# Values of the attention stage in two scaled f16 parts made by VectorE, with a per-head scale found on the chip

## The chip, the cores and the metric

The kernel runs as one program on one NeuronCore of a Trainium2 chip. TensorE (PE) multiplies matrices and adds into PSUM; VectorE (DVE), ScalarE (ACT) and GpSimd (POOL) work element by element; SyncE (SP) issues nearly all transfers of the 16 DMA engines. Each engine works through one queue in order. The metric is device time in microseconds; the kernel before has a median of 976.02 us over three runs (972.43 to 976.55).

## The reference

Attention of 4 batches of 8 heads with 576 tokens and 64 columns per head, causal, with a decay that is a running sum of log f; then two MLPs with a squared ReLU on 2304 tokens, 512 wide, hidden 2048. All inputs are float32.

```
scores = q @ k.T / 8 + cum[:, None] - cum[None, :]      # cum = cumsum(log(clip(f)))
scores = where(causal, -1e9, scores)
attn = exp(scores - max) ; attn = attn / (sum(attn) + 1e-9)
x = (attn @ v) transposed to (2304, 512)
x = relu(x @ w_in)**2 @ w_out        # first MLP
y = relu(x @ w2_in)**2 @ w2_out      # second MLP
```

## The kernel before

**Precision by parts.** A float32 matrix is written as a high part and a low part of a faster type, and three products (high by high, high by low, low by high) are added in PSUM. In attention the probabilities are two f16 parts, and the values v were three parts that together hold all 24 bits: a bf16 part read out of v's own upper half words, and two remainders, made by two subtractions on POOL (`v_parts`, line 448). The product probabilities by values, called AV below (`av`, line 750), then had 15 matmuls per head: five blocks of keys by two probability parts, with a weight of 128 columns that holds two value parts (columns 0 to 63 of the result are folded with columns 64 to 127 afterwards), and five more matmuls with a 64-column weight for the third value part (`THIRD`).

**Stages.** The first 192 tokens of every head go through small shapes (`first_part`, `pair`). The other 384 tokens go through `unit(b, h)`, 32 times, one per batch and head. A unit loads q and k (`raw`), splits them (lines 659 to 674), multiplies scores (line 713), takes maxima (409, DVE), exponents (417, ACT), reciprocals (423, 426), writes the two f16 parts of the probabilities (432 on ACT, 439 on DVE), turns them with one transposing transfer into the single buffer `pt` (line 731, SP), does AV (750) and folds the result into X (766, 768). As there is one `pt`, the transfer of a unit waits until AV of the unit before it is done. v has two buffers, so v of a unit is loaded once AV two units earlier is done.

**The MLPs.** `mlp_a(g)` is the first MLP on 256 tokens (lines 861 and 936: runs of 12 matmuls of 256 columns), nine groups g = 0 to 8. Groups 0 to 2 need only the first 192 tokens of each head, the later ones the units, so these runs fill TensorE between the steps of the units. When the last unit is folded, the second MLP's weights are prepared (`w_in_forms`, `w_out_parts`), and the second MLP (1233, 1259) ends the kernel.

**Order.** Nothing is timed at run time. `Plan.run` lays every engine's queue out beforehand: each step has a priority, a modelled duration and dependencies, and the planner issues on each engine the ready step of lowest priority number. A DMA step is given a modelled landing time. `either(...)` gives a step to whichever of two engines the planner finds free. The q and k load of unit h of the first batch may not start before a step of the first MLP whose number is P10 + P11*h (`TUNE`).

Of the kernel before, what the change touches and what calls it, by code (L numbers as in the profile page):

```python
# [22 lines left out]
NB = 13  # L23
MW = 448

THIRD = ((0, 0), (1, 1), (3, 0), (2, 1), (4, 0))
S15 = 2.0 ** -15


TUNE = dict(  # L30
    AP0=0.0, AP1=201.48, BP0=1647.15, BP1=207.89, P10=15.97, P11=1.88, P20=24.71, P21=3.44, P30=32.76,
    P31=1.6, P40=50, P41=6, PP=917.52, SP0=44.13, SP1=155.02, WP0=-459.53, WP1=133.32, e3=12, e6=6, ev=0,
    f3=2, f4=1, fa=0, fo=20.89, hl=3, kd=0, kl=3, la=0.1, nbo=2, nph=2, npt=1, nqa=3, pha=0, phi=2,
    pq=-119.59, pz=12.35, qd=2, ql=3, sqa=2, sqe=7, vd=-20.75, vr=2, wf=0.59, wl=3, wn=1, wq=2, ws=5,
# [29 lines left out]


class Op:
    __slots__ = ("how", "prio", "uses", "nwait", "ready", "outs", "data", "turn", "dmas", "rows")


class Plan:  # L70
# [14 lines left out]
    def __init__(self):  # L85
        self.ops = []

    def op(self, eng, dur, fn, prio, deps=(), uses=(), data=None, other=None, dmas=1, rows=128):


        o = Op()
        o.how, o.uses, o.data, o.dmas, o.rows, o.turn = {eng: (dur, fn, 0)}, tuple(uses), data, dmas, rows, dur == self.TURN[0]
# [12 lines left out]

    def run(self):
# [5 lines left out]
        lanes, issued = [0.0] * 8, 0  # L112
# [7 lines left out]
        todo = len(self.ops)  # L120
        t, events = 0.0, []
        while todo:
            again = True
            while again:
                again = False
                for e in engs:
# [38 lines left out]
                    if e == "PE":  # L165
# [65 lines left out]
def dve(n):  # L231
    return 0.07 + n / 960.0
# [30 lines left out]
def attention_then_two_squared_relu_mlps(  # L263
# [26 lines left out]
    P = Plan()  # L290
    op = P.op
# [12 lines left out]
    X = base.tile([128, KD, RING], F32, name="X")  # L304
# [11 lines left out]
    st_ = [st[:, 0:1024], st[:, 1024:2048]]  # L316
# [41 lines left out]
    def groups(c0, c1):  # L358
# [4 lines left out]
    ap_ = att_stack.enter_context(tc.tile_pool(name="att", bufs=1))  # L363
# [9 lines left out]
    vv_t = tiles(ap_, 2, [128, 5, 2, D], F32, "vv")  # L373
    VV = Pool(vv_t, True)
    stat = ap_.tile([128, 2, 3, 8], F32, name="stat")
    PP = Pool([(x, stat[:, i, 0], stat[:, i, 1], stat[:, i, 2])
               for i, x in enumerate(tiles(ap_, 2, [128, S], F32, "pp"))], True)

# [24 lines left out]
    all_att = []  # L403
# [39 lines left out]
    def v_parts(vv, n, prio, dep):  # L443


        def rest(eng, i):
            x = vv()[:, :, i]
            eng.tensor_tensor(out=vv()[:, :, 1] if i == 0 else x.bitcast(BF16)[:, :, 0::2], in0=x,  # L448
                              in1=x.bitcast(BF16)[:, :, 1::2], op=ALU.subtract)
# [4 lines left out]
        return dep  # L454

    vv_of = {}

    def first_part(y, prio):

# [183 lines left out]
    def unit(b, h, prio, first):  # L643

        c = QA
        qk_ = [Buf(QK), Buf(QK)]
        ta, tb = qk_
        raw, vv, ph, pT, o = Buf(RAW), Buf(VV), Buf(PH), Buf(PT), Buf(BO)
        vv_of[vv] = vv

        def load_raw():
            nc.sync.dma_start(out=raw(), in_=qk[b, h])
# [41 lines left out]
        ]  # L694

        def load_v():
            nc.sync.dma_start(out=vv()[:, :, 0], in_=v[b, h])

        ov = op("SP", P.COPY[0], load_v, prio + TUNE["vd"], [ld], [vv], data=0.91)
        ov = v_parts(vv, 5, prio + TUNE["vd"], ov)  # L700

        p_ops = []
        for t, blk in PB.items():
            pp = Buf(PP)
            q0, wd = QB[t], QB[t + 1]
            cuts = [(0, wd)] if wd <= 512 else [(0, wd // 2), (wd // 2, wd)]
# [18 lines left out]
            a = (pp, ph, t, 128, 0, wd, blk)  # L725
# [7 lines left out]
        o_tr = op("SP", P.TURN[0], tr, prio, p_ops + (a_av if b == 0 else []), [ph, pT], data=2.9)  # L733


        def av():
            x, w_, z = pT(), vv().bitcast(BF16), o()
            cuts = []
            for j in range(5):
                t = max(2, j)  # L740
                cuts.append((j, slice(QB[t] - QA, S - QA), slice(PB[t] + j, PB[4] + j + 1, 4)))
            todo = []
            for j, q, n in cuts:
                for z0 in range(0, 2 * NB, NB):
                    todo.append((z[:, q], w_[:, j].rearrange("p z d -> p (z d)")[:, 1::2], x[:, n.start + z0:n.stop + z0:n.step]))
# [12 lines left out]
        def fold(eng):  # L758
            s = p0
            rows = slice((h % 2) * 64, (h % 2) * 64 + 64)  # L760
            while s < p1:
                r = s % RING
                n = min(p1 - s, RING - r)
                dst = X[rows, h // 2, r:r + n]
                if eng == "ACT":
                    nc.scalar.mul(out=dst, in_=o()[64:128, s - p0:s - p0 + n], mul=S15)
                else:
                    nc.vector.scalar_tensor_tensor(
                        out=dst, in0=o()[0:64, s - p0:s - p0 + n], scalar=S15, in1=dst, op0=ALU.mult, op1=ALU.add)
# [11 lines left out]
    decoded = []  # L781
# [501 lines left out]
    with tc.manual_schedule():  # L1283
# [97 lines left out]
        o = op("SP", P.COPY[0], f_load, U, data=0.2)  # L1381
# [10 lines left out]
        o = op("DVE", dve2(Q0), lambda: f_clip(0, Q0), U, [o_f])  # L1392
# [20 lines left out]
        def step(n):  # L1413
            return m2_of[0, int(n) // NF, int(n) % NF]

        w_all = []
# [108 lines left out]
```

## Time and profile before

| | |
|---|---|
| median of three runs | 976.02 us (972.43 to 976.55) |
| profiled execution | 977.94 us, its span 976.2 us |
| PE busy | 948.3 us (97%) |
| DVE, ACT, POOL busy | 683.6, 453.1, 361.4 us (70%, 46%, 37%) |
| units: first AV to last AV | 150.84 to 482.62 us |
| TensorE clock | 0.77 of full up to 60 us, 1.00 for most of the rest |

The span counts from the first to the last instruction; the profiled execution has 1.7 us around it. Busy times of an engine are the union of its instructions. A wait is put down to what came last.

### The profile page before, as it was taken

Reading aid. Unit: us, or ns where it says so; the run is one execution under the profiler, and the core shown is the slowest. Engines: PE = TensorE matmul, PEld = TensorE weight load, DVE = VectorE, ACT = ScalarE, POOL = GpSimd, SP = SyncE. Lnnn points to the kernel's source line nnn. Section 1 sums busy time; section 2 is a strip of 40 time slices with the busy share of each in tenths; the row PEclk is TensorE's granted clock in tenths of the full one; section 3 lists DMA queues with packets and bytes.
Section 4 is the critical chain, followed back from the end, with each engine's and each line's share of the span. In section 5 each row is a group of like instructions: output and inputs, shape, how many; then the busy total and the mean of one; then the engine's idle time right before and its main releaser. Section 6 shows DMA issues by size and latency. Waiting matters only on the chain.

```text
span 976.2 us, 17134 instructions
## 1 busy us (share of the span) xinstructions
PE 948.3 (97%) x6463; PEld 866.7 (89%) x6463; DVE 683.6 (70%) x1341; ACT 453.1 (46%) x900; POOL 361.4 (37%) x315
## 2 busy tenths in 40 slices
PE   6999999999999999999999999999999999999997
PEld 3888898999997999999999998988898988989886
DVE  7998667787768778876478689888874445734343
ACT  3686677777777678775333353223230112311011
POOL 2244443444434435434232435332351314522130
PEclk7799999999999999999999999999999999999999
DMA  8767245666656756755546524674452111322113
GB/s 251 253 202 207 83 104 119 140 129 146 132 110 134 148 122 134 143 118 120 120 160 207 173 82 157 199 242 159 134 171 88 64 65 65 117 86 79 65 65 108
DMA packets 177187, 131.91 MB, mean 135 GB/s; under 512 B 140944, under 2 KB 155536, under 8 KB 175056
## 3 DMA queue, kind: packets, MB, share of 16 engines
q1 hardware_dynamic: 176848, 130.32, 49.1%
q8 instruction: 51, 0.84, 0.4%
q10 hardware_dynamic: 256, 0.49, 0.2%
q14 instruction: 32, 0.26, 0.1%
HBM read 85.07 MB, written 18.42 MB: 106 GB/s over the span
## 4 chain that ended last, share of the span: by engine, by line
PE 70%; DVE 11%; issue 9%; POOL 3%; ACT 3%; DMA 2%; POOLq 0%; SPq 0%; ACTq 0%; DVEq 0%
PE yp L936 16%; PE hp L861 16%; PE hp L1233 13%; PE bk L1259 10%; PE bk L750 5%; PE yp L1259 5%; PE bk L713 4%; POOL g L1246 2%; DVE ph L439 1%; DVE tmp L818 1%; DVE tmp L820 1%; DVE pp L409 1%; DVE w L1122 1%; POOL gt L886 1%; DVE w L837 1%
## 5 line engine op out<-in xcount | busy, mean ns | idle before, releaser
L936 PE MATMUL yp<-gt,w 128*128 128x256 f32 x1728 | 231.6, 283 | 1.8 <-POOL gt L886 1.7
L861 PE MATMUL hp<-xk,w 128*128 128x256 f32 x1728 | 227.7, 282 | 1.1 <-DVE w L837 0.8
L936 PEld LDWEIGHTS yp<-gt,w 128*128 128x128 f32 x1728 | 216.5, 189 | 6.2 <-POOL gt L886 3.1
L861 PEld LDWEIGHTS hp<-xk,w 128*128 128x128 f32 x1728 | 215.3, 190 | 3.0 <-DVE w L837 1.0
L886 POOL TENSOR_TENSOR gt<-sq,gt 128x512 fp32r<-128x512 f32 x72 | 97.3, 1352 | 154.4 <-ACT gt L883 135.9
L1259 PE MATMUL bk<-w,g 128*128 128x512 f32 x576 | 148.5, 394 | 0.7 <-POOL g L1246 0.7
L1246 POOL TENSOR_TENSOR g<-r,g 128x768 fp32r<-128x768 f32 x36 | 66.8, 1855 | 203.2 <-ACT g L1245 199.3
L1233 PE MATMUL hp<-w 128*128 128x384 f32 x630 | 123.9, 335 | 0.1
L1259 PEld LDWEIGHTS bk<-w,g 128*128 128x128 f32 x576 | 106.6, 188 | 18.7 <-POOL g L1246 1.6
L1245 ACT CAST g<-r 128x768 fp32r<-128x768 f32 x47 | 39.3, 835 | 180.1 <-DVE r L1244 180.0
L1233 PEld LDWEIGHTS hp<-w 128*128 128x128 f32 x630 | 111.7, 188 | 8.1 <-DVE st L1210 0.4
L417 ACT ACTIVATE pp<-pp,stat 128x448 f32<-128x448 f32 (+1 forms) x128 | 78.4, 613 | 44.6 <-DVE stat L409 37.0
L439 DVE SCALAR_TENSOR_TENSOR ph<-pp,stat,ph 128x320 f16<-128x320 f32 (+2 forms) x96 | 77.3, 814 | 15.5 <-ACT ph L432 13.9
L1210 DVE TENSOR_TENSOR r<-hp,st 128x384 f32<-128x384 f32 x62 | 34.5, 556 | 62.8 <-PE hp L1233 62.7
L448 POOL TENSOR_TENSOR vv<-vv 128x320 f32<-128x320 f32 x64 | 54.4, 850 | 54.8 <-DMA vv<-in_v_dram 42.1
L1244 DVE SCALAR_TENSOR_TENSOR r<-r 128x768 f32<-128x768 f32 x47 | 73.6, 1567 | 1.4
L1259 PE MATMUL yp<-w,g 128*128 128x512 f32 x288 | 74.5, 393 | 0.0
L1233 PE MATMUL hp<-w,far 128*128 128x384 f32 x378 | 74.1, 335 | 0.0
L870 ACT ACTIVATE sq<-hp 128x512 f32<-128x512 f32 x72 | 42.8, 594 | 66.8 <-PE hp L861 66.3
L1233 PEld LDWEIGHTS hp<-w,far 128*128 128x128 f32 x378 | 67.3, 188 | 4.7
L409 DVE CUSTOM_DVE_ANT_0 pp<-bk,mask 128x448 f32<-128x448 f32 (+1 forms) x128 | 59.4, 476 | 15.3 <-PE bk L713 9.9
L873 DVE SCALAR_TENSOR_TENSOR sq<-hp,sq 128x512 f32<-128x512 f32 x64 | 44.0, 688 | 35.1 <-ACT sq L870 34.7
(171 smaller groups left out, 1281.5 us busy)
## 6 DMA issues: line engine op xcount, KB each, us to landing
w<-wo_d SPq DMA_DIRECT2D x48, 512.0 KB
stage<-in_w_dram SPq DMA_DIRECT2D x26, 512.0 KB
raw<-in_qk_dram SPq DMA_DIRECT2D x32, 288.0 KB
wo_d<-part SPq DMA_DIRECT2D x16, 512.0 KB
ph<-in_w_dram SPq DMA_DIRECT2D x7, 1024.0 KB
st<-in_w_dram SPq DMA_DIRECT2D x6, 1024.0 KB
vv<-in_v_dram SPq DMA_DIRECT2D x32, 160.0 KB
qk_a<-in_qk_dram SPq DMA_DIRECT2D x16, 192.0 KB
```

The costliest lines, as they stand in the source:

```text
L409: nc.vector.tensor_tensor_reduce(out=x[:rows, c0:c0 + wd], in0=src, in1=msk, scale=-0.125, scalar=3.0e38 if first else nmax[:rows, 5:6], o ...
L417: nc.scalar.activation(out=x, in_=x, func=AF.Exp, scale=-1.0, bias=nmax[:rows, t:t + 1], accum_out=ssum[:rows, t:t + 1])
L439: nc.vector.scalar_tensor_tensor(out=flat[:rows, z:z + wd], in0=x, scalar=r, in1=flat[:rows, 128 * blk:128 * blk + wd], op0=ALU.mult, op1= ...
L448: eng.tensor_tensor(out=vv()[:, :, 1] if i == 0 else x.bitcast(BF16)[:, :, 0::2], in0=x, in1=x.bitcast(BF16)[:, :, 1::2], op=ALU.subtract)
L750: nc.tensor.matmul(dst.rearrange("p (n c) -> p n c", n=rh.shape[1]), lhsT=lt, rhs=rh, start=(i == 0), stop=(i == len(todo) - 1), skip_grou ...
L861: nc.tensor.matmul(ps, lhsT=lt, rhs=rh, start=(k_ == 0 and c == 0), stop=(k_ == KD - 1 and c == 2))
L886: eng.tensor_tensor(out=gt[1]()[:, :c], in0=sq()[:, :c], in1=f32(gt[0]()[:, :c]), op=ALU.subtract)
L936: nc.tensor.matmul(yp[d // 2]()[:, d % 2], lhsT=lt, rhs=rh, start=(i == 0 and c == 0 and d % 2 == 0), stop=(i == NF - 1 and c == 2), skip_ ...
L1233: nc.tensor.matmul(ps()[:, 0:TH], lhsT=lt, rhs=rh, start=(k_ == 0 and c == 0), stop=(k_ == 1 and c == 2))
L1244: o = op("DVE", dvs(TU), lambda r=r: nc.vector.scalar_tensor_tensor(out=r(), in0=r(), scalar=0.0, in1=r(), op0=ALU.max, op1=ALU.mult), e0, ...
L1246: l = either_vp(TU, lambda e, r=r, g=g: e.tensor_tensor(out=g()[:, 1], in0=r(), in1=f32(g()[:, 0]), op=ALU.subtract), e0, [h], [r, g])
L1259: nc.tensor.matmul(bank(ob[c]), lhsT=g()[:, a, c * 128:(c + 1) * 128], rhs=rw()[:, b], start=(p == 0 and x == 0 and z == 0), stop=(p == NP ...
```

## The change

v is written as two f16 parts. So that f16's range suffices, each head is first scaled by a power of two found from its largest magnitude: `scales(b)` loads all of v of a batch (2560 columns on 128 partitions, in five pieces; three for the first batch), takes the maximum of each row on DVE, stores 128 maxima to DRAM, reads them back onto all partitions, and in six small DVE steps makes a scale up and a scale down for each head. A unit's `v_parts` is then two DVE steps (multiply and round to f16; multiply and subtract). AV loses its five 64-column matmuls, and the two fold steps multiply with the scale down in place of the constant. The planner's DMA steps get an extra modelled landing time `lag`: 4 us for the pieces and for the reading back, 8 us for the store. P10 goes from 15.97 to 12.

```diff
-    AP0=0.0, AP1=201.48, BP0=1647.15, BP1=207.89, P10=15.97, P11=1.88, ...
+    AP0=0.0, AP1=201.48, BP0=1647.15, BP1=207.89, P10=12, P11=1.88, ...
...
-                            end = lanes[issued % 8] = dma + self.LAT["DMA"] + (self.TURNED if o.turn else 0.0)
+                            end = lanes[issued % 8] = dma + self.LAT["DMA"] + (self.TURNED if o.turn else 0.0) + o.lag
...
-        for i in range(2):
-            dep = either(TUNE["vr"], ("POOL", pool_(n * D), lambda i=i: rest(nc.gpsimd, i)),
-                         ("DVE", dvs(n * D), lambda i=i: rest(nc.vector, i)), prio, [dep], [vv_of[vv]])
+        def hi():
+            nc.vector.tensor_scalar(out=parts_v(vv)[:, :, 0], in0=x(), scalar1=up, scalar2=None, op0=ALU.mult)
+
+        def lo():
+            nc.vector.scalar_tensor_tensor(out=parts_v(vv)[:, :, 1], in0=x(), scalar=up, in1=parts_v(vv)[:, :, 0], op0=ALU.mult, op1=ALU.subtract)
+
+        o = op("DVE", dve(5 * D) + 0.07, hi, prio, [dep, scale_of[b]], [vv])
+        return op("DVE", dvs(5 * D) + 0.08, lo, prio, [o], [vv])
...
+    def scales(b, prio, pieces, space, deps):
...
+            o = op("SP", P.COPY[0], load, prio, deps + [os_[j - 2] if j > 1 else None], data=n * 0.00143, lag=4.0)
+            os_.append(op("DVE", dve(n), top_of, prio, [o]))
...
+        o = op("DVE", 0.08, lambda: nc.vector.tensor_reduce(out=top[:, 7:8], in_=top[:, 0:k], op=ALU.max, axis=mybir.AxisListType.X), prio, os_)
+        o = op("SP", P.COPY[0], lambda: nc.sync.dma_start(out=top_d[b].rearrange("(p o) -> p o", o=1), in_=top[:, 7:8]), prio, [o], data=0.05, lag=8.0)
+        o = op("SP", P.COPY[0], lambda: nc.sync.dma_start(out=space, in_=top_d[b:b + 1].to_broadcast([128, 128])), prio, [o], data=0.2, lag=4.0)
...
+        for y in range(6):
+            o = op("DVE", 0.2 if y == 0 else 0.08, lambda y=y: step(y), prio, [o])
+        scale_of[b] = o
...
-            for i, half in THIRD:
-                j, q, n = cuts[i]
-                todo.append((z[64 * half:64 * half + 64, q], w_[:, j, 1, 0::2], x[:, n]))
...
-        o_av = op("PE", 1.65, av, prio, [o_tr, ov] + gone, [pT, vv, o])
+        o_av = op("PE", 1.35, av, prio, [o_tr, ov] + gone, [pT, vv, o])
...
+        scales(0, TUNE["BP0"] - 40.0, early, X[:, 2, 768:896], [decoded[14]] + aug_second)
...
+        scales(1, 3850.0, later, st_[1][:, 512:640], w_all + [all_att[-8]])
```

The batches 2 and 3 have such a call each. The line numbers of the changed kernel are 52 to 55 higher from `pair` on (AV is line 802, the folds 818 and 820), and 2 higher in `max_of` to `p_lo`.

The queues move at three places. First TensorE, at the end of AV of the first unit (`bk` is the PSUM result, `pt` the turned probabilities, `vv` the values; the last figure of a row is weight columns by moving columns). Before:

```order
L750 MATMUL bk_89<-pt_101,vv_103 128x128
L750 LDWEIGHTS vv_103
L750 MATMUL bk_89<-pt_101,vv_103 64x384
L750 LDWEIGHTS vv_103
L750 MATMUL bk_89<-pt_101,vv_103 64x384
L750 LDWEIGHTS vv_103
L750 MATMUL bk_89<-pt_101,vv_103 64x256
L750 LDWEIGHTS vv_103
L750 MATMUL bk_89<-pt_101,vv_103 64x384
L750 LDWEIGHTS vv_103
L750 MATMUL bk_89<-pt_101,vv_103 64x128
L936 MATMUL yp_93<-gt_79,w 128x256
```

and now:

```order
L802 MATMUL bk_90<-pt_102,vv_104 128x128
L802 LDWEIGHTS vv_104
L802 MATMUL bk_90<-pt_102,vv_104 128x128
L913 MATMUL hp_92<-xk_86,w 128x256 x6
L913 MATMUL hp_92<-xk_84,w 128x256 x6
```

The five 64-column products are gone and a run of the first MLP stands right behind the ten that stay; what else follows differs because the planner chose another filler there.

Second VectorE, where the first units begin (`w` is the first MLP's last weight, `xk` the split of X for its next group, `qk` the split of k, `sq` the MLP's square, `top` the row maxima). Before:

```order
L837 TENSOR_TENSOR w<-ph,w 128x2x512
L913 TENSOR_TENSOR xk_83<-X,xk_83 128x512
L913 TENSOR_TENSOR xk_84<-X,xk_84 128x512
L873 SCALAR_TENSOR_TENSOR sq_77<-hp_91,sq_77 128x512
L952 COPY st<-yp_94 128x512
L873 SCALAR_TENSOR_TENSOR sq_78<-hp_92,sq_78 128x512
L665 TENSOR_TENSOR qk_1230<-raw,qk_1229 64x576
L674 CAST qk_1230<-qk_1229 64x384
```

and now, there and some 55 rows further on:

```order
L889 TENSOR_TENSOR w<-ph,w 128x2x512
L483 TENSOR_REDUCE top<-X 128x1 x2
L965 TENSOR_TENSOR xk_84<-X,xk_84 128x512
L965 TENSOR_TENSOR xk_85<-X,xk_85 128x512
L720 TENSOR_TENSOR qk_1239<-raw,qk_1238 64x576
L729 CAST qk_1239<-qk_1238 64x384
...
L508 TENSOR_SCALAR up_down<-up_down 128x8
L459 TENSOR_SCALAR vv_104<-vv_104,up_down 128x5x64
L459 TENSOR_SCALAR vv_105<-vv_105,up_down 128x5x64
L462 SCALAR_TENSOR_TENSOR vv_104<-vv_104,up_down 128x5x64
L462 SCALAR_TENSOR_TENSOR vv_105<-vv_105,up_down 128x5x64
L441 SCALAR_TENSOR_TENSOR ph<-pp_109,stat,ph 128x320
```

The split of the first unit's k has moved ahead of two squares and an evacuation, two reductions stand before it, and the four value steps stand in the row of the probability parts. In the later units the two value steps of a unit follow its last probability part (441) closely.

Third SyncE, in the same place (`y_d` the first MLP's output, `top_d` the maxima in DRAM). Before:

```order
L652 DMA raw<-in_qk_dram 128x576
L957 DMA y_d<-st 128x2x64 x8
L697 DMA vv_103<-in_v_dram 128x5x64
L652 DMA raw<-in_qk_dram 128x576
L697 DMA vv_104<-in_v_dram 128x5x64
L652 DMA raw<-in_qk_dram 128x576 x2
L731 DMA_TRANSPOSE pt_101<-ph 128x26x128
```

and now:

```order
L707 DMA raw<-in_qk_dram 128x576
L480 DMA X<-in_v_dram 128x2x256
L707 DMA raw<-in_qk_dram 128x576
L752 DMA vv_104<-in_v_dram 128x320
L752 DMA vv_105<-in_v_dram 128x320
L492 DMA top_d<-top 128x1
L707 DMA raw<-in_qk_dram 128x576
L1009 DMA y_d<-st 128x2x64 x8
L493 DMA X<-top_d 128x128
L786 DMA_TRANSPOSE pt_102<-ph 128x26x128
```

The loads of the second and third unit and the store of the maxima now stand ahead of the eight stores of the MLP's first group, and the reading back stands between those and the first transposing transfer.

## Rows read from the trace of the kernel before

**Rows 1.** Page: span and busy time of each engine.
```profile
span 976.2 us, 17134 instructions
PE 948.3 (97%) x6463; PEld 866.7 (89%) x6463; DVE 683.6 (70%) x1341; ACT 453.1 (46%) x900; POOL 361.4 (37%) x315
```
**Rows 2.** Busy time by stretch: PE, PEld, DVE, ACT, POOL, clock, DMA share, GB/s.
```profile
128.00:485.00 357.00, 352.63 (x2830) 323.53 (x2829) 263.07 (x717) 255.01 (x527) 151.77 (x145) 1.00 0.61 130
330.00:485.00 155.00, 155.00 (x1266) 143.05 (x1265) 108.22 (x288) 104.48 (x216) 65.06 (x62) 1.00 0.61 128
```
**Rows 3.** Timeline of TensorE, first and last units: start, duration, line, operation, count.
```profile
150.84 1.93 PE L750 MATMUL bk<-pt,vv 128*128 128x384 f16 x15
152.70 1.69 PE L936 MATMUL yp<-gt,w 128*128 128x256 f32 x12
...
161.74 1.93 PE L750 MATMUL bk<-pt,vv 128*128 128x384 f16 x15
...
481.21 1.57 PE L936 MATMUL yp<-gt,w 128*128 128x256 f32 x12
482.62 1.93 PE L750 MATMUL bk<-pt,vv 128*128 128x384 f16 x15
```
**Rows 4.** Timeline of TensorE, end of one AV: its five 64-column products.
```profile
439.72 0.52 PE L750 MATMUL bk<-pt,vv 128*64 128x384 f16 x5
440.17 3.09 PE L936 MATMUL yp<-gt,w 128*128 128x256 f32 x24
```
**Rows 5.** Timeline of SyncE's queue over the first units.
```profile
105.51 0.61 SPq L652 DMA_DIRECT2D raw<-in_qk_dram  x1
123.85 4.82 SPq L957 DMA_DIRECT2D y_d<-st  x8
...
129.36 0.62 SPq L652 DMA_DIRECT2D raw<-in_qk_dram  x1
...
152.81 3.90 SPq L731 DMA_TRANSPOSE pt<-ph  x1
156.76 0.59 SPq L697 DMA_DIRECT2D vv<-in_v_dram  x1
```
**Rows 6.** What the transposing transfers waited for in SyncE's queue: total us, times, longest.
```profile
SPq L731 <- PE hp L861: 42.7, 8, 7.4
SPq L731 <- PE bk L713: 41.1, 8, 7.8
SPq L731 <- PE bk L750: 29.6, 13, 4.3
SPq L731 <- DVE ph L439: 18.0, 8, 5.4
```
**Rows 7.** Groups by form: count, busy us, mean ns of one, idle before.
```profile
L448 POOL TENSOR_TENSOR vv<-vv 128x320 bf16<-128x320 f32 x32 | 28.9, 903 | 1.9
L448 POOL TENSOR_TENSOR vv<-vv 128x320 f32<-128x320 f32 x32 | 25.5, 796 | 53.0 <-DMA vv<-in_v_dram 42.1 <-PE bk L713 10.0 <-PE hp L861 0.7
L439 DVE SCALAR_TENSOR_TENSOR ph<-pp,stat,ph 128x320 f16<-128x320 f32 x32 | 24.3, 759 | 3.1 <-ACT ph L432 1.8
L674 DVE CAST qk<-qk 64x384 fp32r<-64x384 f32 x32 | 15.0, 468 | 0.3
L423 DVE TENSOR_SCALAR stat<-stat 128x1 f32<-128x1 f32 x96 | 14.5, 151 | 19.7 <-ACT pp L417 19.2
L498 DVE TENSOR_REDUCE tmp<-tmp 128x8 f32<-128x512 f32 x2 | 1.4, 679 | 0.0
```
**Rows 8.** Line 439 by itself: durations min, median, max in ns.
```profile
L439 DVE SCALAR_TENSOR_TENSOR ph<-pp,stat,ph x96: 534/789/1527, 134.3 to 471.7; 128x320 f16<-128x320 f32 x32, 128x448 f16<-128x448 f32 x32, 128x576 f16<-128x576 f32 x32
```
**Rows 9.** Timeline of VectorE before the first unit; in brackets the idle time before.
```profile
116.21 1.73 DVE L913 TENSOR_TENSOR xk<-X,xk 128x512 fp32r<-128x512 f32 x2 [3.12 <-ACT xk L909]
...
128.13 1.33 DVE L665 TENSOR_TENSOR qk<-raw,qk 64x576 fp32r<-64x576 f32 x1 [1.38 <-ACT qk L662]
```
**Rows 10.** Timeline of POOL: the first value step of the third unit.
```profile
159.88 0.72 POOL L448 TENSOR_TENSOR vv<-vv 128x320 f32<-128x320 f32 x1 [1.27 <-DMA vv<-in_v_dram]
```

More of the change, by code (lines that the diff above doesn't have):

```diff
@@ L66 @@
 class Op:
-    __slots__ = ("how", "prio", "uses", "nwait", "ready", "outs", "data", "turn", "dmas", "rows")
+    __slots__ = ("how", "prio", "uses", "nwait", "ready", "outs", "data", "turn", "dmas", "rows", "lag")
 class Plan:
@@ L86, in __init__, with op @@
         self.ops = []
-    def op(self, eng, dur, fn, prio, deps=(), uses=(), data=None, other=None, dmas=1, rows=128):
+    def op(self, eng, dur, fn, prio, deps=(), uses=(), data=None, other=None, dmas=1, rows=128, lag=0.0):
         o = Op()
-        o.how, o.uses, o.data, o.dmas, o.rows, o.turn = {eng: (dur, fn, 0)}, tuple(uses), data, dmas, rows, dur == self.TURN[0]
+        o.how, o.uses, o.data, o.dmas, o.rows, o.turn, o.lag = {eng: (dur, fn, 0)}, tuple(uses), data, dmas, rows, dur == self.TURN[0], lag
         if other:
@@ L375, in attention_then_two_squared_relu_mlps @@
     stat = ap_.tile([128, 2, 3, 8], F32, name="stat")
+    top = ap_.tile([128, 8], F32, name="top")
+    up_down = ap_.tile([128, B, 2, H], F32, name="up_down")
     PP = Pool([(x, stat[:, i, 0], stat[:, i, 1], stat[:, i, 2])
@@ L440, in p_lo @@
             out=flat[:rows, z:z + wd], in0=x, scalar=r, in1=flat[:rows, 128 * blk:128 * blk + wd], op0=ALU.mult, op1=ALU.subtract)
[L443 to L449, printed above, removed]
-        for i in range(2):
-            dep = either(TUNE["vr"], ("POOL", pool_(n * D), lambda i=i: rest(nc.gpsimd, i)),
-                         ("DVE", dvs(n * D), lambda i=i: rest(nc.vector, i)), prio, [dep], [vv_of[vv]])
-        return dep
@@ L456, in attention_then_two_squared_relu_mlps, with raw_v, parts_v, v_parts @@
-    vv_of = {}
+    def raw_v(vv):
+        return vv().rearrange("p n z d -> p (n z d)")[:, 0:5 * D]
+    def parts_v(vv):
+        return vv().rearrange("p n z d -> p (n z d)")[:, 5 * D:].bitcast(F16).rearrange("p (n z d) -> p n z d", n=5, z=2)
+    def v_parts(vv, b, h, prio, dep):
+        up = up_down[:, b, 0, h:h + 1]
+        def x():
+            return raw_v(vv).rearrange("p (n d) -> p n d", d=D)
+        def hi():
[4 more added lines that the diff above has]
+        return op("DVE", dvs(5 * D) + 0.08, lo, prio, [o], [vv])
@@ new lines, in attention_then_two_squared_relu_mlps, with load, top_of, step @@
+    scale_of = {}
+    def scales(b, prio, pieces, space, deps):
+        src = v[b].rearrange("h (y q) n d -> (h y) (q n d)", y=128 // H)
+        c, os_, last = 0, [], [None] * len(pieces)
+        for j, x in enumerate(pieces):
+            n = 1
+            for y in x.shape[1:]:
+                n *= y
+            def load(x=x, c=c, n=n):
+                s_ = src[:, c:c + n]
+                nc.sync.dma_start(out=x, in_=s_.rearrange("p (a c) -> p a c", a=x.shape[1]) if len(x.shape) == 3 else s_)
+            def top_of(x=x, j=j):
+                nc.vector.tensor_reduce(out=top[:, j:j + 1], in_=x, op=ALU.max, axis=mybir.AxisListType.XY if len(x.shape) == 3 else mybir.AxisListType.X,
+                                        apply_absolute_value=True)
+            o = op("SP", P.COPY[0], load, prio, deps + [os_[j - 2] if j > 1 else None], data=n * 0.00143, lag=4.0)
+            os_.append(op("DVE", dve(n), top_of, prio, [o]))
+            c += n
+        assert c == src.shape[1]
+        k = len(pieces)
+        o = op("DVE", 0.08, lambda: nc.vector.tensor_reduce(out=top[:, 7:8], in_=top[:, 0:k], op=ALU.max, axis=mybir.AxisListType.X), prio, os_)
+        o = op("SP", P.COPY[0], lambda: nc.sync.dma_start(out=top_d[b].rearrange("(p o) -> p o", o=1), in_=top[:, 7:8]), prio, [o], data=0.05, lag=8.0)
+        o = op("SP", P.COPY[0], lambda: nc.sync.dma_start(out=space, in_=top_d[b:b + 1].to_broadcast([128, 128])), prio, [o], data=0.2, lag=4.0)
+        m, up, down = up_down[:, b, 1], up_down[:, b, 0].bitcast(U32), up_down[:, b, 1].bitcast(U32)
+        def step(y):
+            if y == 0:
+                nc.vector.tensor_reduce(out=m, in_=space.rearrange("p (h y) -> p h y", h=H), op=ALU.max, axis=mybir.AxisListType.X)
+            elif y == 1:
+                nc.vector.tensor_scalar(out=m, in0=m, scalar1=1.0e-27, scalar2=None, op0=ALU.max)
+            elif y == 2:
+                nc.vector.tensor_scalar(out=down, in0=down, scalar1=0x7F800000, scalar2=None, op0=ALU.bitwise_and)
+            elif y == 3:
+                nc.vector.tensor_scalar(out=up, in0=down, scalar1=0x7F800000, scalar2=None, op0=ALU.bitwise_xor)
+            elif y == 4:
+                nc.vector.tensor_scalar(out=up_down[:, b, 0], in0=up_down[:, b, 0], scalar1=2.0 ** 13, scalar2=None, op0=ALU.mult)
+            else:
+                nc.vector.tensor_scalar(out=m, in0=m, scalar1=2.0 ** -29, scalar2=None, op0=ALU.mult)
+        for y in range(6):
+            o = op("DVE", 0.2 if y == 0 else 0.08, lambda y=y: step(y), prio, [o])
+        scale_of[b] = o
@@ L648, in unit @@
         raw, vv, ph, pT, o = Buf(RAW), Buf(VV), Buf(PH), Buf(PT), Buf(BO)
-        vv_of[vv] = vv
         def load_raw():
@@ L696, in load_v @@
         def load_v():
-            nc.sync.dma_start(out=vv()[:, :, 0], in_=v[b, h])
+            nc.sync.dma_start(out=raw_v(vv), in_=v[b, h].rearrange("p n d -> p (n d)"))
         ov = op("SP", P.COPY[0], load_v, prio + TUNE["vd"], [ld], [vv], data=0.91)
-        ov = v_parts(vv, 5, prio + TUNE["vd"], ov)
+        ov = v_parts(vv, b, h, prio + TUNE["vd"], ov)
         p_ops = []
@@ L736, in av @@
         def av():
-            x, w_, z = pT(), vv().bitcast(BF16), o()
+            x, w_, z = pT(), parts_v(vv), o()
             cuts = []
@@ L744, in av @@
                 for z0 in range(0, 2 * NB, NB):
-                    todo.append((z[:, q], w_[:, j].rearrange("p z d -> p (z d)")[:, 1::2], x[:, n.start + z0:n.stop + z0:n.step]))
-            for i, half in THIRD:
-                j, q, n = cuts[i]
-                todo.append((z[64 * half:64 * half + 64, q], w_[:, j, 1, 0::2], x[:, n]))
+                    todo.append((z[:, q], w_[:, j].rearrange("p z d -> p (z d)"), x[:, n.start + z0:n.stop + z0:n.step]))
             for i, (dst, lt, rh) in enumerate(todo):
@@ L765, in fold @@
                 if eng == "ACT":
-                    nc.scalar.mul(out=dst, in_=o()[64:128, s - p0:s - p0 + n], mul=S15)
+                    nc.scalar.activation(out=dst, in_=o()[64:128, s - p0:s - p0 + n], func=AF.Copy, scale=up_down[64:128, b, 1, h:h + 1])
                 else:
                     nc.vector.scalar_tensor_tensor(
-                        out=dst, in0=o()[0:64, s - p0:s - p0 + n], scalar=S15, in1=dst, op0=ALU.mult, op1=ALU.add)
+                        out=dst, in0=o()[0:64, s - p0:s - p0 + n], scalar=up_down[0:64, b, 1, h:h + 1], in1=dst, op0=ALU.mult, op1=ALU.add)
                 s += n
@@ L1423, in attention_then_two_squared_relu_mlps @@
         opened = op("POOL", 0.01, open_qk, TUNE["BP0"] - 1.0, a_tr + [o_ph])
+        early = [X[:, :, 768:1024], X[:, :, 0:256], X[:, 0:2, 768:1024]]
+        later = [st_[j % 2][:, 512:1024] for j in range(5)]
+        scales(0, TUNE["BP0"] - 40.0, early, X[:, 2, 768:896], [decoded[14]] + aug_second)
         for h in range(H):
@@ L1430, in attention_then_two_squared_relu_mlps @@
         mlp_a(5)
+        scales(2, 5350.0, later, st_[1][:, 512:640], w_all + [all_att[-8]])
         for h in range(H):
@@ L1433, in attention_then_two_squared_relu_mlps @@
         mlp_a(6)
+        scales(3, 6850.0, later, st_[1][:, 512:640], w_all + [all_att[-8]])
         for h in range(H):
```

4 lines of the change are left out of this document (2 added, 2 removed).

## The prediction

> **What bounds the kernel now.** I read the page first: TensorE is busy for 948.3 of 976.2 us [rows 1]. A share of the whole span says little about one stage, so next come the sums by stretch. The units, which are all that the change touches, lie between 128 and 485 us. There TensorE stands idle for 357 - 352.6 = 4.4 us, and between 330 and 485 us for nothing; VectorE is busy for 263 of 357 us, 74% [rows 2]. The reader is to see that in this stage TensorE never runs out of work, because runs of the first MLP fill every hole between the steps of the units, at full clock.
>
> Then the timeline. From the first AV at 150.84 to the last at 482.62 us there are 31 periods, 331.8 / 31 = 10.70 us per unit [rows 3]. Two things could set that period. One is TensorE's own queue, which is full. The other is the ring around the single buffer `pt`: the transposing transfer is issued at 152.81, right after the first AV ended at 152.70, and the next AV starts at 161.74, 8.9 us later, and takes 1.86 us [rows 3, 5]. 8.9 + 1.9 = 10.8 is about the period too. So the planner has balanced both, and a shorter AV shortens both by the same amount. That is why I do not have to decide between them.
>
> **The five products that go.** In one AV the five 64-column matmuls start at 439.72, and the next work starts at 440.17 us: 0.45 us [rows 4]. Their count of columns would suggest more, but two of them run beside others in the two halves of the array, and the rows have that in them. The whole AV, 152.70 - 150.84 = 1.86 us [rows 3], becomes 1.41 us. 32 units x 0.45 = 14.4 us of TensorE's time, all in a stage where TensorE waits for 4.4 us in all. The two f16 parts keep the 128 weight columns and the type's width, so the ten products that stay cost what they cost now.
>
> By the Trainium skill's page "Perfetto Trace Analysis", section "Identifying the Most-Contended Engine", the busy share of matmuls is a poor measure of how near TensorE is to its limit, and the share of weight loads a better one. Here that share is 143.05 of 155 us, 92%, in the fullest stretch [rows 2]; if only so much of the 14.4 us were real, 13.3 us would be left. I go by the rows that start back to back.
>
> **What VectorE gets.** Per unit one multiplication of 320 columns into f16 and one multiply and subtract of 320 columns. The second has the shape of line 439's 320-column form: 0.53 us at its fastest, 0.76 us in the mean [rows 7, 8]. The first has one tensor source, as the copy of 384 columns, 0.47 us in the mean [rows 7]; I bound it by 0.3 and 0.76. Together 0.83 to 1.52 us, and I take 1.0 us: 32 us in all. The maxima: 2560 columns per batch, at 0.68 us per 512 columns [rows 7] 3.4 us, with four batches 13.6 us. Seven small steps per batch at 0.15 us [rows 7]: 4 us. Sum 50 us (bounds 44 and 66).
>
> What leaves: 28.9 + 25.5 = 54 us of POOL's work [rows 7]. Line 439's 320-column form takes 0.76 us in the mean against 0.53 at best, and up to 1.5 [rows 8]; part of that spread is POOL working at the same time, so VectorE gets some time back. Its whole spread is 32 x 0.23 = 7 us; I take 5, between 0 and 7.
>
> So VectorE has 263 + 50 - 5 = 308 us of work. Its time: the stage shrinks by 14.4 us and begins sooner. In the queue the first unit's k split now follows the two X splits, which stood at 116.21 us, instead of 128.13 [rows 9]: some 10 us. 357 - 14.4 + 10 - 6 (the end moves further forward, below) = 347 us. 308 / 347 = 89%. Per unit that is 9.6 us of work in a period of 10.70 - 0.45 = 10.25 us. This fits, with 0.6 us to spare, where before it had 2.5. That narrow room is the main risk.
>
> **Why I still expect the order to hold.** The transposing transfers mostly waited for TensorE (42.7, 41.1 and 29.6 us), and for the last probability part of VectorE 18.0 us in 8 cases [rows 6]: VectorE was ahead of the ring. In the new queue the two value steps follow the last probability part, where VectorE has this lead, and AV needs them only one period later. For what the smaller lead costs I take half of the stage's present idle time again, 2.2 us, between -4.4 (all of it goes) and the rivals below.
>
> **The start.** Loads of 1.3 MB stand before the first units. They are issued where SyncE now loads `raw` at 105.51 us and then sits until 123.85 us behind the stores of `y_d`; the second `raw` went only at 129.36 us [rows 5]. Now three unit loads go before those stores. The two reductions fall into a hole of 3.1 us before the X split [rows 9], and take 2.7 us there. I cost the start at nothing. The printed order has 47 runs of MLP products ahead of the first AV where there were 51, 4 x 1.41 = 5.6 us sooner (a run takes 482.62 - 481.21 = 1.41 us [rows 3]), and 17 behind the last AV where there were 12; these cover the folds and the split for group 7, with 5 x 1.41 = 7 us more than now. After the units TensorE is full as before, and the preparation of the second MLP's weights keeps its distance to TensorE.
>
> **Sum.** 977.94 us of the profiled execution - 14.4 + 2.2 = 965.7; this execution lies 1.9 us above the median of 976.02, so the median to be measured is 963.8 us, rounded 964. Its own range is 957 (14.4 and 4.4 saved) to 971. What a measurement of this kernel can tell from no change is about 0.5%, 4.9 us.
>
> **Rivals.**
> *VectorE becomes the bound, level.* If in-order waits add 1.0 us per unit to the 9.6 us, the period is 10.65 us and 0.05 x 32 is all that is won: about 975 us. For it: 89% in an engine that waits for TensorE, ScalarE and transfers in one queue. Against it: the 26% of idle time that it has now is largely caused by the ring, not by its own load. Chance 0.13.
>
> *v's landing waits move from POOL to VectorE, slower.* POOL waited 42.1 us for the landing of v [rows 7]. v is issued only when the transposing transfer's 4 us in SyncE's queue are over (152.81, 156.76 [rows 5]) and its first step starts at 159.88, 3.1 us later, after an idle wait for it [rows 10]. On POOL little stood behind this; on VectorE the next unit's maxima, the MLP's squares and the probability parts do. If VectorE waits as POOL did, 42.1 / 32 = 1.3 us per unit, the period is 9.6 + 1.3 = 10.9 us, 0.65 us over what TensorE needs: 32 x 0.65 = 21 us, 976 - 14.4 + 21 = 983 us. It decides once the waits pass 0.6 us per unit. Against it: the value steps stand behind the last probability part, so VectorE comes to them later than POOL did. Chance 0.11.
>
> *The scale comes late.* The reading back of the maxima stands before the first transposing transfer, and VectorE's queue has six steps that wait for it. If it landed 5 us late in each of the four batches, VectorE would stall 20 us; the first 7 us are covered by the longer tail of filler, and the other batches have a stretch of queue between store and reading back: some 6 us would reach the end, 970 us. Chance 0.05.
> The Trainium skill's page "DMA: Bandwidth & Descriptors" puts a transfer's fixed cost near 2 us (section "Anatomy of one DMA — SWDGE (gpsimd) path") and the smallest piece for full rate at 512 bytes (section "Specifications"); the store of maxima has 4-byte pieces. Two such transfers in four batches would be 16 us if nothing hid them. No row here shows a 4-byte store.
>
> The forecast itself has 0.71. Faster by over 0.5% (under 971 us): 0.71 + 0.05 and nothing of the level case, 0.76. Within: 0.13. Slower: 0.11. The range takes in the forecast, the late scale and the way towards the level case: 957 to 974 us.
>
> **What would show it.** In the new profile: AV takes 1.41 us from its start to the next work, 32 times; the first AV lies near 145 us and the last near 462; TensorE's idle time between them stays under 7 us; VectorE is busy for close to 90% there, POOL for some 54 us less; the period is 10.2 us. The forecast is wrong if TensorE's gaps in the units grow by more than 9 us, with VectorE's queue as their releaser, or if VectorE stands idle before lines 459 or 498 for a landing by more than 20 us in all.

## The result, and the profile after

The changed kernel takes 985.71 us (median, 981.75 to 987.69), the one before 974.32 us in the same session: a ratio of 1.0111 [1.0067, 1.0155], 1.1% slower and clear of noise. The forecast was 964.0 us, faster. The profiled execution took 987.01 us.

The page first, against [rows 1]: span, then busy time by engine.

```profile
span 984.9 us, 16859 instructions
PE 935.7 (95%) x6303; PEld 862.3 (88%) x6303; DVE 726.7 (74%) x1451; ACT 461.4 (47%) x901; POOL 311.2 (32%) x250
```

TensorE has 12.6 us less to do and the span is 8.7 us longer: TensorE waits now. Two sums by stretch (columns as in [rows 2]), the first over the same 357 us as there:

```profile
128.00:485.00 357.00, 334.72 (x2597) 312.50 (x2597) 291.71 (x803) 255.42 (x512) 94.36 (x77) 0.98 0.67 139
115.00:490.00 375.00, 351.58 (x2731) 328.21 (x2730) 304.86 (x832) 266.08 (x533) 101.18 (x83) 0.98 0.66 136
```

TensorE's idle time there is 357 - 334.7 = 22.3 us where it was 4.4. From here on "the gaps" are TensorE's idle time from 115 to 490 us: 375 - 351.6 = 23.4 us now, and 375 - 370.5 = 4.5 us in the kernel before, whose row is

```profile
115.00:490.00 375.00, 370.51 (x2980) 341.21 (x2978) 268.61 (x726) 261.00 (x536) 156.13 (x148) 1.00 0.59 125
```

VectorE is busy for 82%, so it is not full. What TensorE waited for between 115 and 490 us (total us, times, longest):

```profile
PE bk L768 <- DMA qk<-aug_d: 11.9, 3, 4.8
PE bk L768 <- DVE stat L425: 3.5, 4, 1.2
PE bk L768 <- DVE stat L411: 2.4, 6, 0.7
PE bk L768 <- ACT xk L961: 1.4, 1, 1.4
```

Half of it is three waits of the scores for a transfer of 15 KB (the augmented rows of q and k, line 710). The forecast did not speak of that transfer. The first of the three on TensorE's timeline:

```profile
126.69 0.30 PE L768 MATMUL bk<-qk 128*128 128x320 f32 x1
131.83 1.38 PE L768 MATMUL bk<-qk 68*128 68x320 f32 x3 [4.83 <-DMA qk<-aug_d]
```

and what SyncE and ScalarE issued and waited for at that time:

```profile
121.51 0.33 SPq L492 DMA_DIRECT2D top_d<-top  x1
121.93 0.38 SPq L707 DMA_DIRECT2D raw<-in_qk_dram  x1
122.91 10.62 SPq L1009 DMA_DIRECT2D y_d<-st  x8
133.58 0.47 SPq L493 DMA_DIRECT2D X<-top_d  x1
```

```profile
122.55 0.25 ACTq L710 DMA_DIRECT2D qk<-aug_d  x1
132.75 0.67 ACT L717 CAST qk<-raw 64x576 fp32r<-64x576 f32 x1 [7.99 <-DMA raw<-in_qk_dram]
```

Everything issued just behind the store of the maxima (121.51) is late: the eight stores of `y_d` hold SyncE for 10.62 us where they took 4.82 [rows 5], the augmented rows issued at 122.55 let TensorE go on only at 131.83, and ScalarE sits for 7.99 us before the `raw` issued at 121.93. The sums by stretch over these 16 us (the last three columns are granted clock, DMA share, GB/s):

```profile
122.00:126.00 4.00, 3.99 (x34) 3.93 (x34) 3.59 (x14) 2.42 (x7) 0.49 (x1) 1.00 1.05 22
126.00:133.00 7.00, 2.17 (x12) 1.86 (x11) 0.52 (x2) 0.25 (x1) 0.00 (x0) 0.83 0.57 83
133.00:138.00 5.00, 5.00 (x27) 4.99 (x26) 3.60 (x12) 4.36 (x10) 1.94 (x2) 0.55 0.23 50
```

Behind the store the DMA engines are fully occupied (share 1.05) and move 22 GB/s, against 139 GB/s over the whole stage. After the gap the granted clock falls towards its lower level, 1.2 GHz (0.55 in the last stretch). By the single clock records it is low for 6.8 us at this gap and for 3.4 us at each of the other two, 13.6 us in all, where the kernel before has 3.4 us in the stage. The extra 10.2 us at half speed cost about 5.1 us; this is an estimate.

So gaps +18.9, clock +5.1, against what AV saves. That saving is larger than forecast:

```profile
150.94 1.48 PE L802 MATMUL bk<-pt,vv 128*128 128x384 f16 x10
152.23 2.96 PE L913 MATMUL hp<-xk,w 128*128 128x256 f32 x23
```

152.23 - 150.94 = 1.29 us against 1.86 [rows 3], 0.57 us per unit, 18.2 us in all.

In sum + 18.9 + 5.1 - 18.2 = 5.8 us. The two profiled executions lie 9.1 us apart (977.94 and 987.01); 2.4 us of what is left is idle time of TensorE outside of 115 to 490 us. The medians lie 11.4 us apart, because the profiled execution of the kernel before is 3.6 us above its median here, 974.32, and that of the changed kernel 1.3 us above its own.

The value steps in VectorE's groups of the stage (columns as in [rows 7]), against POOL's there:

```profile
L462 DVE SCALAR_TENSOR_TENSOR vv<-vv,up_down 128x320 f16<-128x320 f32 x32 | 20.2, 633 | 0.2
L441 DVE SCALAR_TENSOR_TENSOR ph<-pp,stat,ph 128x320 f16<-128x320 f32 x32 | 18.3, 573 | 0.7 <-ACT ph L434 0.6
L459 DVE TENSOR_SCALAR vv<-vv,up_down 128x320 f16<-128x320 f32 x32 | 17.1, 538 | 0.8 <-DMA vv<-in_v_dram 0.6
```

The two steps take 1.17 us per unit and wait for v's landing for 0.6 us in the whole stage.

### The profile page after: what moved, and what is told of

Its sections match the earlier page's. It is cut to its first block, busy times and chain, and to the rows that moved or that the text cites. A ratio compares the mean times of both kernels' runs of the same rounds, so it can differ in the third digit from the quotient of the medians.

```text
span 984.9 us, 16859 instructions
## 1 busy us (share of the span) xinstructions
PE 935.7 (95%) x6303; PEld 862.3 (88%) x6303; DVE 726.7 (74%) x1451; ACT 461.4 (47%) x901; POOL 311.2 (32%) x250
## 4 chain that ended last, share of the span: by engine, by line
PE 35%; issue 8%; DVE 4%; DMA 3%; POOL 3%; ACT 1%; POOLq 0%; SPq 0%; DVEq 0%; ACTq 0%
PE hp L1285 13%; PE bk L1311 10%; PE yp L1311 5%; PE yp L988 3%; PE hp L913 3%; DMA stage<-in_w_dram 3%; POOL g L1298 2%; DVE w L1174 1%; DVE word L1125 1%; DVE sq L925 0%; PE bk L802 0%; POOL gt L938 0%; ACT w L1172 0%; DVE X L1154 0%; DVE lw L1125 0%
## 5 line engine op out<-in xcount | busy, mean ns | idle before, releaser
L988 PEld LDWEIGHTS yp<-gt,w 128*128 128x128 f32 x1728 | 218.8, 191 | 6.2 <-POOL gt L938 5.2
L768 PE MATMUL bk<-qk 68*128 68x288 f32 (+5 forms) x256 | 63.2, 343 | 22.0 <-DMA qk<-aug_d 11.9
L441 DVE SCALAR_TENSOR_TENSOR ph<-pp,stat,ph 128x320 f16<-128x320 f32 (+2 forms) x96 | 72.3, 759 | 8.3 <-ACT ph L434 7.4
L723 POOL TENSOR_TENSOR qk<-raw,qk 64x384 fp32r<-64x384 f32 x32 | 35.0, 1093 | 126.0 <-ACT qk L714 108.1
L434 ACT ACTIVATE ph<-pp,stat 128x320 f16<-128x320 f32 (+2 forms) x96 | 63.1, 665 | 18.5 <-DVE stat L428 10.4
```

Of the source, the lines that this page charges most:

```text
L434: nc.scalar.activation(out=a, in_=x, func=AF.Copy, scale=r)
L441: nc.vector.scalar_tensor_tensor(out=flat[:rows, z:z + wd], in0=x, scalar=r, in1=flat[:rows, 128 * blk:128 * blk + wd], op0=ALU.mult, op1= ...
L768: nc.tensor.matmul(bk()[:, 0:c1 - c0], lhsT=x()[:rows, q0 - QA:wd - QA], rhs=x()[:rows, NQ + c0:NQ + c1], start=(y == 0), stop=(y == 1), s ...
L988: nc.tensor.matmul(yp[d // 2]()[:, d % 2], lhsT=lt, rhs=rh, start=(i == 0 and c == 0 and d % 2 == 0), stop=(i == NF - 1 and c == 2), skip_ ...
```

## The experiments

Times are medians, ratios are to the kernel before on the same chip. All versions of the changed kernel in the first group keep the order of all matmuls, and of VectorE's, ScalarE's and POOL's steps apart from the few left out. So a different order explains none of their differences.

**1. The store, the reading back, and both.** Three versions of the changed kernel.

```diff
# gathered row: 128 maxima into one row of SBUF, then one store of 512 bytes
-nc.sync.dma_start(out=top_d[b].rearrange("(p o) -> p o", o=1), in_=top[:, 7:8])
+nc.sync.dma_start(out=line_, in_=top[:, 7:8])
...
+nc.sync.dma_start(out=top_d[b:b + 1], in_=line_)
 nc.sync.dma_start(out=space, in_=top_d[b:b + 1].to_broadcast([128, 128]))
# neither store nor reading back: both left out, m set to 0.5
# store only: reading back left out, m set to 0.5
```

> The changed kernel with the same planned order; the 128 maxima of a batch are first gathered into one row of SBUF and stored to DRAM as one piece of 512 bytes, in place of 128 pieces of 4 bytes. Theory S (the 4-byte store to DRAM holds up the transfers behind it): the three long TensorE gaps behind lines 768 and aug_d (4.8, 4.6, 2.4 us) and the clock drops after them go, 12 + 5 = 17 us, about 969 us. Theory V (VectorE at 83% with a narrow room is what costs): within 4 us of the changed kernel's 986. If 4-byte pieces into one SBUF partition are as bad, also 986.

> The changed kernel with the same planned order; v is loaded and its row maxima are taken, but they are neither stored nor read back, and the scale comes from the constant 0.5. Leaves out the scale of each head. Theory S: 967 to 970 us, as e1 or 1 us less. Theory V: 982 to 986 us.

> The changed kernel with the four stores of the maxima kept as they are (128 pieces of 4 bytes side by side in DRAM) and the reading back left out; the scale is a constant, so the maxima aren't used. Theory: the store alone stalls the transfers behind it, so nearly the whole distance from the version without store and reading back (974.1) to the changed kernel (985.7) stays, 982 to 987 us, with long waits of the scores for the augmented rows (aug_d) after each store. Rival: the reading back does it, by its place ahead of the first transposing transfer; then about 974 to 977 us and no such waits.

| version | us | ratio | gaps, us |
|---|---|---|---|
| changed kernel | 985.71 | 1.0111 [1.0067, 1.0155] | 23.4 |
| store only | 984.21 | 1.0107 [1.0081, 1.0134] | 21.6 |
| neither | 974.10 | 0.9994 [0.9980, 1.0008] | 13.9 |
| gathered row | 971.79 | 0.9966 [0.9952, 0.9981] | 13.8 |

The sums from 115 to 490 us on which the gaps of the last three rest, and TensorE's waits for the augmented rows, each time in the order store only, neither, gathered row:

```profile
115.00:490.00 375.00, 353.45 (x2770) 330.45 (x2769) 305.62 (x834) 265.56 (x532) 101.73 (x83) 0.99 0.65 134
115.00:490.00 375.00, 361.10 (x2849) 338.07 (x2848) 313.37 (x845) 269.85 (x539) 104.96 (x85) 1.00 0.63 138
115.00:490.00 375.00, 361.20 (x2857) 338.81 (x2856) 313.36 (x845) 270.34 (x540) 105.86 (x86) 1.00 0.64 140
```

```profile
PE bk L768 <- DMA qk<-aug_d: 12.3, 5, 5.1
PE bk L768 <- DMA qk<-aug_d: 5.2, 5, 1.5
PE bk L774 <- DMA qk<-aug_d: 5.3, 4, 1.4
```

The store alone brings back 10.1 of the 11.6 us between "neither" and the changed kernel; by the ratios, which take out the difference of the chips, 11.0 of 11.4. That is what its theory said. "Neither" itself missed: 974.10 us lies 4 us above the 967 to 970 that was expected. The timelines of the store alone look like those of the changed kernel:

```profile
119.41 0.33 SPq L492 DMA_DIRECT2D top_d<-top  x1
119.83 0.38 SPq L707 DMA_DIRECT2D raw<-in_qk_dram  x1
120.82 10.48 SPq L1009 DMA_DIRECT2D y_d<-st  x8
```

```profile
130.03 1.38 PE L768 MATMUL bk<-qk 68*128 68x320 f32 x3 [5.13 <-DMA qk<-aug_d]
```

With the gathered row the same eight stores, issued right behind 128 pieces of 4 bytes that go into SBUF, take 4.95 us (4.84 in "neither"), and the later 512-byte store and the reading back add no gaps (13.8 against 13.9 us):

```profile
119.56 0.55 SPq L498 DMA_DIRECT2D X<-top  x1
120.20 0.54 SPq L713 DMA_DIRECT2D raw<-in_qk_dram  x1
120.97 4.95 SPq L1015 DMA_DIRECT2D y_d<-st  x8
125.97 0.32 SPq L494 DMA_DIRECT2D top_d<-X  x1
127.20 0.34 SPq L495 DMA_DIRECT2D X<-top_d  x1
```

This version computes what the changed kernel computes and is faster than both, by 0.2 to 0.5% against the kernel before. It is also 2.3 us under "neither", which does less. The difference does not come from TensorE's waits: in the two profiled executions TensorE is idle for 39.5 us of the span, and busy for 929.1 us with the gathered row and 932.8 in "neither", at a granted clock of 0.90 and 0.87 before 115 us. Why the clock differs there was not tried.

**2. The store in the kernel before.** Is it the smallness of the pieces, or where they lie? Four such stores that nothing reads were added behind the loads of the fourth head.

```diff
             nc.sync.dma_start(out=raw(), in_=qk[b, h])
+            if h == 3:   # apart: each piece 512 bytes from the next
+                nc.sync.dma_start(out=junk_d[b, :, 0:1], in_=mask[:, 0:2].bitcast(F32))
# side by side: junk_d[b] is 128 floats, out=junk_d[b].rearrange("(p o) -> p o", o=1)
```

> The kernel before, with one more transfer in each batch, right behind the unit load of head 3: 4 bytes from each of 128 partitions to DRAM, which nothing reads. Theory S: late landings behind each, two to four TensorE gaps of 2 to 5 us with clock drops, 982 to 992 us. Theory V: no change, 974 to 976 us.

> As the run with four extra 4-byte stores in the kernel before, but the 128 pieces of a store lie side by side in 512 bytes of DRAM (as the changed kernel's maxima do), not 512 bytes apart. Theory S2 (pieces of 4 bytes in one and the same stretch of DRAM hold up what follows): late landings behind each store, gaps of 2 to 5 us, 980 to 990 us. Theory W (the store is harmless; what cost was a wait of SyncE's queue or the reading back): 974 to 976 us.

Apart: 975.37 us, ratio 1.0008 [0.9994, 1.0021]. Side by side: 982.46 us, 1.0070 [1.0048, 1.0092]. Only the place in DRAM differs. SyncE behind the second store, apart and then side by side:

```profile
221.12 0.43 SPq L655 DMA_DIRECT2D junk_d<-mask  x1
222.79 0.33 SPq L653 DMA_DIRECT2D raw<-in_qk_dram  x1
225.32 3.98 SPq L734 DMA_TRANSPOSE pt<-ph  x1
```

```profile
222.82 0.42 SPq L655 DMA_DIRECT2D junk_d<-mask  x1
224.04 0.33 SPq L653 DMA_DIRECT2D raw<-in_qk_dram  x1
226.57 7.89 SPq L734 DMA_TRANSPOSE pt<-ph  x1
```

The transposing transfer takes 7.89 us in place of 3.98, and AV waits for it. By stretch, apart and side by side:

```profile
224.50:231.00 6.50, 6.49 (x53) 5.91 (x52) 3.92 (x15) 4.20 (x10) 1.01 (x1) 1.00 0.78 160
```

```profile
225.00:231.50 6.50, 6.50 (x54) 5.84 (x52) 3.71 (x12) 4.04 (x8) 1.48 (x2) 1.00 1.23 51
```

So 4-byte pieces as such cost nothing measurable here; 128 of them into the same 512 bytes of DRAM slow the transfers behind them, 51 against 160 GB/s in these stretches, and the four stores cost 982.46 - 974.89 = 7.6 us. The four do not act alike: the transposing transfers behind them take 4.63, 7.89, 3.96 and 6.94 us side by side, and 4.04, 3.98, 3.96 and 4.55 us apart. Behind the second and the fourth store a load of `raw` goes out before the transposing transfer, behind the other two none; whether this makes the difference was not tried, nor was any distance between 4 and 512 bytes. By the Trainium skill's page "DMA: Bandwidth & Descriptors", section "Rules for kernel authors", many small transfers should be made into one large one. That rule is about transfers, and here it is the pieces of one transfer; carried over to them, the runs agree for pieces side by side (985.71 to 971.79 us when gathered) and not for pieces 512 bytes apart (975.37 against 974.20 us).

**3. The saving alone, and the values without the maxima.** The kernel before without its five products, order kept (the third value part is left out of the result); and the changed kernel without loads, reductions, store and reading back (the scale is a constant).

```diff
# kernel before
-            for i, half in THIRD:
-                j, q, n = cuts[i]
-                todo.append((z[64 * half:64 * half + 64, q], w_[:, j, 1, 0::2], x[:, n]))
# changed kernel: load, top_of, store, reading back do nothing; m set to 0.5
```

> The kernel before without the five 64-column products of each unit (leaves out the third value part), all else and the planned order kept. The 0.45 us per unit of the prediction: 975 - 14.4 = 960 to 962 us. If the ring around pt or VectorE set the pace instead of TensorE, less than half of that: 968 to 975 us.

> The changed kernel's planned order with v's extra loads, the reductions, the store and the reading back all not issued; constant scale (leaves out the scale of each head). What is left of the change: two value steps on VectorE, ten products, the planner's order. Theory M (the 5.2 MB of loads and 13 us of reductions crowd the units): unit gaps fall from 13.8 to about 6 us, 964 to 967 us. Theory V (the value steps in VectorE's queue make the small gaps): 969 to 974 us, as without the round trip alone.

The first takes 966.61 us, ratio 0.9919 [0.9896, 0.9942]: 7.6 us from 974.2, although AV is 0.57 us shorter in 32 units, 18.2 us. It lies between the two ranges of its expectation. Its gaps are 375 - 365.29 = 9.7 us:

```profile
115.00:490.00 375.00, 365.29 (x2897) 342.61 (x2898) 274.33 (x736) 262.21 (x538) 159.70 (x150) 1.00 0.61 128
```

```profile
PE bk L713 <- DVE stat L409: 4.6, 6, 2.0
PE bk L713 <- DMA qk<-aug_d: 2.7, 3, 1.5
```

and the same two waits in the kernel before:

```profile
PE bk L713 <- DVE stat L409: 2.3, 3, 1.4
PE bk L713 <- DMA qk<-aug_d: 1.2, 3, 0.5
```

With TensorE quicker, the scores come to VectorE's maxima (409) and to the augmented rows before these are done: 5.2 us come back as gaps, 3.8 of them in these two waits, although VectorE has no new work. The rest, 18.2 - 5.2 - 7.6 = 5.4 us, is mostly no loss of this version: the profiled execution of the kernel before is 3.7 us above the median on that chip, 974.20 us, and from one profiled execution to the other 977.94 - 966.38 = 11.6 us are won. That leaves 1.4 us, against 2.1 us more idle time of TensorE before 115 us.

The second takes 970.70 us, 0.9952 [0.9931, 0.9973], gaps 12.4 us, as theory V had it and not theory M: 4.1 us over the first (3.2 by the ratios), for the values on VectorE and the new order together, and 3.4 us under "neither" (4.1 by the ratios), for the maxima's loads and reductions.

**4. Sooner attention.** The gathered row with other values of P10; each is a new order.

```diff
-P10=12
+P10=15.97   # and 8, and 10
```

> The version with one row of SBUF and one 512-byte store (971.8 us), with P10 back at 15.97, so that the units begin as late as in the kernel before. If the sooner start is worth what the prediction gave it (7 us more cover at the end), 973 to 979 us and gaps near the last units; if it is worth nothing, 970 to 973 us.

> The version with the maxima gathered in one row and stored as 512 bytes (971.8 us), with P10 = 8 in place of 12. Theory: from 15.97 to 12 gave 17 us since the first units came sooner and the filler behind the last unit grew; if sooner is better still, 966 to 971 us. Rival: the first loads are bound by what stands before them by now, and the units come no sooner: 970 to 974 us, or more where the new order has longer gaps.

> As the one before, with P10 = 10. Theory (sooner is better): 968 to 972 us. Rival (each P10 is another order of the whole stage, whose gaps scatter by several us whatever the start): anything from 968 to 985 us, with first AV within 2 us of 141.7 and the difference in the sum of TensorE's gaps.

| P10 | us | ratio | first AV at | gaps, us |
|---|---|---|---|---|
| 8 | 985.48 | 1.0119 [1.0098, 1.0140] | 146.15 | 20.0 |
| 10 | 980.60 | 1.0071 [1.0050, 1.0092] | 144.10 | 16.7 |
| 12 | 971.79 | 0.9966 [0.9952, 0.9981] | 141.71 | 13.8 |
| 15.97 | 988.92 | 1.0146 [1.0116, 1.0176] | 145.28 | 22.6 |

From 15.97 and 12 alone one would say that a sooner start is worth 17 us, as the expectation for 8 did (that for 15.97 had been 970 to 979 us, and was missed by 10). It is wrong: 8 and 10 are slower again, and time goes with the gaps, not with P10. The rival for 10 said so, though it had the first AV within 2 us of 141.7, and it came 2.4 us later. The number picks one of many orders, and their gaps scatter by 9 us. With 15.97 one wait of the scores is for VectorE's split of k:

```profile
388.34 0.83 PE L774 MATMUL bk<-qk 68*128 68x320 f32 x3 [3.61 <-DVE qk L735]
```

**5. The first value part on ScalarE** (gathered row, newly planned).

```diff
-o = op("DVE", dve(5 * D) + 0.07, hi, prio, [dep, scale_of[b]], [vv])
+o = op("ACT", act(5 * D) + 0.09, hi_act, prio, [dep, scale_of[b]], [vv])
```

> The version with one row of SBUF, and the first value part (multiply and round to f16) on ScalarE in place of VectorE, newly planned. It takes some 16 us of VectorE's 50 away and gives ScalarE 18 us. Theory V: gaps fall by 3 to 5 us, 966 to 969 us. If TensorE's wait is for ScalarE or transfers as much as for VectorE: 970 to 975 us.

978.23 us, 1.0034 [1.0019, 1.0050]; gaps 11.8 us, so 2 us less, but 5.4 us in place of 1.8 from 490 to 960 us, and the time is above both ranges that were expected. The order changed too, and after experiment 4 this can't be told apart from the move.

## Why the prediction was wrong

- **The start, "I cost the start at nothing": the step that failed.** The loads and reductions nearly did fit (3.4 us in all batches, experiment 3), and the store was judged by SyncE's queue alone. The same store in the three later batches had no term in the sum at all. What it does to transfers behind it had no row, and I gave it no bound. It is worth 13.9 us (985.71 to 971.79 with the row gathered; 10.1 between "store only" and "neither"): in gaps 23.4 - 13.8 = 9.6 us, in clock about 5.1 us. Up to 115 us, ahead of the store, the granted clock of the profiled executions is 0.87 in the changed kernel and 0.90 with the gathered row, and in the other pair 0.90 with the store only and 0.87 with neither; so the store's worth is likely to lie between the two figures. The first AV, forecast near 145, came at 150.94 because of the first gap; with the gathered row it came at 141.71. The last, forecast near 462, came at 485.10, and at 468.82 with the gathered row.
- **"The scale comes late", 970 us, 0.05.** The right place, the wrong mechanism. The value steps waited for nothing (0.8 us idle); q, k and their augmented rows were late, behind three of the four stores, and TensorE with them. The 16 us for two transfers in each batch priced each by itself; the first store holds SyncE for 0.33 us only, and the cost lay in what was issued behind it. "No row here shows a 4-byte store" should have become a range, not a low chance.
- **"For what the smaller lead costs I take half", 2.2 us.** Mis-sized. Without the store's harm the gaps grow from 4.5 to 13.8 us, by 9.3. Of these, 5.2 us come with a shorter AV alone (experiment 3). The period, forecast at 10.2 us, is (468.82 - 141.71) / 31 = 10.55 us. So "a shorter AV shortens both by the same amount" failed. By the waits that grew, a third chain, scores to maxima to the next scores, does not pass through AV, and [rows 6] already had the scores in front of the transposing transfers, 41.1 us.
- **Five products, 0.45 us.** Mis-sized the other way: 0.57 us, 18.2 us in all. From their first start to the next work [rows 4] understates what they cost: the ten that stay end 0.12 us sooner without them. Why was not tried.
- **VectorE, 308 of 347 us.** Near: with the gathered row it is 288 of 341 us (84%, forecast 89%) from 128 to 469 us. The values cost 1.17 us for 1.0, the 320-column step fell from 0.76 to 0.57 us and gave back 6 us for the 5 taken. POOL lost 50 us for 54.
- **The rivals.** VectorE as the bound did not come (82% busy). The landing waits of v did not move to it: 0.6 us against 42.1 on POOL, as argued from their place in the queue. The sign of being wrong, gaps up by more than 9 us, came; its releaser, VectorE's queue, was named wrongly for half of it.

In numbers: 963.8 forecast, - 3.8 (AV), + 7.1 (gaps) = 967.1 us; the gathered row measures 971.8, which is 4.7 us more. The forecast counts from 976.02 us; from the 974.20 us of the kernel before on the chip of the gathered row it is 6.5 us more. Of these, 3.7 us are the distance of the profiled execution of the kernel before from that median, and 2.0 us are idle time of TensorE before 115 us. The changed kernel lies 13.9 us above the gathered row, at 985.7; that is the store, with what the clock ahead of it adds.

## What to carry to other kernels

A transfer's price can lie less in its own time than in what is queued behind it in the DMA engines, as here: for a kind of store that the trace does not show, count the transfers that follow and bound their delay, or gather the pieces in SBUF first. When TensorE is busy for 99% of a stage, other chains may stand close behind it, so do not count the whole saving: here 7.6 of 18.2 us were won by the medians, 11.6 by the two profiled executions. In a kernel whose order a planner lays out, compare versions with the same order, and try a number on both sides before its effect is called a trend.

## What the runs showed of the hardware

Four stores of 128 pieces of 4 bytes side by side in 512 bytes of DRAM cost 7.6 us in the kernel before, the same pieces 512 bytes apart nothing measurable (1.0008 [0.9994, 1.0021]). Packets of other transfers behind such a store took up to 8.2 us each (26 over 1.2 us behind the first store of the changed kernel, all of a `raw` load). From 115 to 490 us the traces have 138 packets of over 1.2 us in the changed kernel and 138 with the store alone, against 72 with neither and 73 with the gathered row; in the kernel before it is 16, with four stores apart 26, and side by side 130. So the same 128 pieces written into one SBUF row added none. Why writes to neighbouring bytes of DRAM hold up other transfers was not tried.
